# Warming matmuls in the first head, the third head's split a head later, and low parts and gather products in another order at the end of attention

## The chip, the cores and the metric

One core of a Trainium2 chip runs the whole program. The metric is the device time of one execution in microseconds (us), the median of three runs.

## The reference

Three layers are chained, all in float32. First comes an attention in which a query sees only the keys whose six sign bits agree with its own; then a mixture of eight experts, one expert for each token; then a gated block.

```python
q_bucket = np.sum(((q @ proj) > 0) * powers, axis=-1)       # 6 bits; the same for k
scores = scale * np.matmul(q, k.transpose(0, 1, 3, 2))
scores = np.where(q_bucket == k_bucket, scores, -1e9)
attn = softmax(scores) ; x = attn @ v                       # 2 x 8 heads, 768 x 64
e_idx = np.argmax(x @ w_gate, axis=1)                       # 1536 tokens, 8 experts
out[mask] = gate_w * eom * (np.maximum(x[mask] @ w1[e], 0.0) @ w2[e])
return ((out @ w_a) * (out @ w_b)) @ w_out
```

## The kernel before

**Heads and tiles.** Sixteen heads run one after the other, each in six tiles of 128 queries against 768 keys. A running number g counts the tiles of all heads, six to a head: tile 0 is the first of head 0, tile 6 the first of head 1, tile 12 the first of head 2. One turn of the loop over g emits, in this order: scores of tile g+1 (`scores`, lines 158 and 159), their row minimum and from it scale and bias of the exponential (`smax`, mm in line 164 and sb in line 165, on DVE), then work named below, then the transposes of tile g (`tposes`, line 186) in two halves, each copied from PSUM by ACT (line 190) or DVE (line 192). The exponential (`sexp`, line 173) runs on ACT and stands at one of three places of the turn, chosen by a table. Two PSUM buffers hold scores, two hold transposes. The product with v of a head (`av_step`, line 201) runs in the tiles of the next head, so head 0 has none.

**Buckets in the scores.** The bucket comparison rides in the scores' matmul: each head's tiles tq and tk hold 64 rows of q or k, rounded, and twelve rows of codes (64 to 75) that add a large number where bits agree. The residuals stand in bq and bk. A head is prepared in these steps: load x (q and k) and v by SyncE's DMA queue (`load`, lines 96 and 98, called three heads ahead in tile 1 of a head); `split_a` rounds q to tq and k to tk on ACT (line 103); `split_b` makes bq on DVE (line 115) with a POOL cast (line 116), and bk on POOL (lines 118 and 119); `hash_mm` (line 128) multiplies x by the projection; `hash_codes` makes all codes in one DVE row (code, line 142), and four DMAs of SyncE carry them into tq and tk (line 147). There are two x buffers: head h's x goes where head h-2's was.

**What sets the order.** It is written out by hand; each engine and SyncE's queue run their rows in the order of emission, and waits are put in where data or a buffer's reuse ask for them. The dictionary K (line 25) holds the places: 'sa' and 'sb' name tile and place of the two `split_a` and `split_b` calls for the head two ahead, 'sa0' and 'sb0' the same for heads 0 and 1; 'ev', 'ev0', 'ev1' say for each half of a tile whether ACT (0) or DVE (1) copies the transposes. `hash_codes(h + 1)` stands in tile 1 of head h. Small POOL copies into `held` only hold POOL's queue until a given row is done.

**The end of attention.** Expert 0's tokens are gathered on TensorE: tokens of the second half are multiplied by one-hot rows (`x0_hot`, `x0_add`, lines 399 and 406) into two PSUM tiles, one for columns 0 to 255 and one for 256 to 511; `x_split` prepares high and low parts of the tokens (lines 375 and 376, xh); `x0_evac` (lines 418 and 419) makes xh and xl for the first expert product `mm1` (lines 903 to 905). In between the router (`router`) finds each token's expert (rows rt_..., oh, ohl on DVE) and its slot by counting matmuls (lines 285 to 292), and POOL scatters the tokens to DRAM (line 428). `heat(n)` issues n small matmuls whose result is not used; the kernel before calls it ahead of tile 0 only.

Of the kernel before, what the change touches and what calls it, by code (L numbers as in the profile page):

```python
# [7 lines left out]
F32 = mybir.dt.float32  # L8
# [5 lines left out]
ALU = mybir.AluOpType  # L14
# [6 lines left out]
NT = 6  # L21
N, DM, E, FF, F2 = 1536, 512, 8, 1024, 1536
C = 224
GR = ((0, 6), (6, 4), (10, 2))
K = {'se': (2, 0, 2, 0, 2, 0), 'se0': (0, 1, 2, 1, 1, 2), 'ev': (0, 0, 0, 1, 0, 1, 0, 0, 0, 0, 1, 0), 'ev0': (0, 0, 0, 1, 0, 1, 0, 0, 0, 1, 0, 0), 'ev1': (0, 0, 0, 1, 0, 1, 0, 0, 0, 1, 0, 1), 'avl': (5,), 'oul': 0, 'hml': 0, 'hc': ((0, 0), (0, 2), (1, 1), (2, 1)), 'sa': ((0, 2), (2, 2)), 'sb': ((1, 0), (2, 2)), 'sa0': ((2, 2), (4, 1)), 'sb0': ((3, 2), (5, 0)), 'ext': (1, 0, 2, 4, 7, 8), 'hm0': 0, 'hc0': ((1, 0), (1, 2), (3, 0), (4, 1))}
C_ID, C_TRI, C_THR, C_REV, C_TOK, C_IOTA, C_BASE, C_SLOT = 0, 128, 256, 258, 266, 278, 279, 287
CW = C_SLOT + C
FAR = 1024.0
# [4 lines left out]
def attn_moe_kernel(ctx: ExitStack, tc: tile.TileContext, xin, cst, projd, wblk, wmoe, w2in, out):  # L33
    nc = tc.nc
    PE, ACT, DVE, POOL = nc.tensor, nc.scalar, nc.vector, nc.gpsimd
# [13 lines left out]
    wl = big.tile([128, 80], F32, name="wl")  # L49
# [38 lines left out]
    NHD = NB * NH  # L88
# [18 lines left out]
    def split_b(h, i, lo=0, n=S):  # L107
        copy = POOL.tensor_copy if h or i else ACT.copy
        x = X[h][:, i * S + lo:i * S + lo + n]
        if lo == 0:  # L110
            B[h, i] = tb.tile([128, S], F32R, tag="b" + "qk"[i], name="b" + "qk"[i])
        b = B[h, i][:, lo:lo + n]
        t = T[h, i].bitcast(F32)[:, lo:lo + n]
        if i == 0:
            DVE.scalar_tensor_tensor(out=b[:64], in0=x[:64], scalar=-0.125, in1=t[:64], op0=ALU.mult, op1=ALU.subtract)
            copy(b[64:], t[64:])  # L116
        else:
            (POOL if h else DVE).tensor_tensor(out=b[64:], in0=x[64:], in1=t[64:], op=ALU.subtract)
            copy(b[:64], t[:64])
# [247 lines left out]

    slot_of, XH = {}, {}

    def x_split(d, t0=6, n=6):  # L370
        if d not in XH:
            XH[d] = [tb.tile([128, 6, 128], F32R, tag="tb"[i] + "qk"[d % 2], name="xh") for i in range(2)]
        h, l = (a[:, t0 - 6:t0 - 6 + n] for a in XH[d])
        x = x_all[:, t0:t0 + n, d * 128:(d + 1) * 128]
        ACT.activation(h, x, ACTF.Copy)
        POOL.tensor_tensor(out=l, in0=x, in1=h.bitcast(F32), op=ALU.subtract)

    x0 = {}

# [222 lines left out]
    with tc.manual_schedule():  # L602
# [18 lines left out]
        DVE.tensor_scalar(out=pst[:, 6:12], in0=pst[:, 0:6], scalar1=-1.0, scalar2=None, op0=ALU.mult)  # L621
        DVE.tensor_scalar(out=pst[:, 32:38], in0=pst[:, 38:44], scalar1=-1.0, scalar2=None, op0=ALU.mult)
        warm = ps_t.tile([128, 512], F32, tag="t", name="warm")
        def heat(n):
            for i in range(n):
                PE.matmul(warm[:, :128], ones, ones, start=True, stop=True)

        heat(44)
        hash_mm(0, (2, 3))
# [22 lines left out]
        def set_up(k):  # L652
            if k == 0:
                split_b(1, 0)
                POOL.tensor_copy(held, pt_[0][:, 0:1])
            elif k == 1:
                split_b(1, 1)
            elif k == 2:
                POOL.memset(oh, 0.0)
                zero = wraw.tile([128, 512], F32, tag="wr0", name="zero")  # L660
                POOL.memset(zero, 0.0)
                zeros.append(zero)
                DVE.tensor_copy(tri, cs[:, C_TRI:C_TRI + 128])
            elif k == 5:
                DVE.tensor_scalar(
                    out=tokc.bitcast(I32)[:, :, 0], in0=cs[:, C_TOK:C_TOK + 12], scalar1=-float(E * C), scalar2=None,
                    op0=ALU.add,
                )
                DVE.tensor_scalar(
                    out=base2, in0=cs[:, C_BASE:C_BASE + 8], scalar1=1.0 / 128, scalar2=None, op0=ALU.mult  # L670
                )
# [3 lines left out]
        L = NHD - 1  # L675
# [7 lines left out]
        for g in range(NG):  # L683
            h, t = divmod(g, NT)
            if t == 1 and h + 3 < NHD:
                load(h + 3)
            if g + 1 < NG:
                scores(g + 1)
                smax(g + 1)
            if g < NT:  # L690
                set_up(g)
            if 2 * NT <= g < 2 * NT + (E * C + N) // 256:
                for i in (g - 2 * NT,):
                    nc.sync.dma_start(
                        out=xr[i * 256:(i + 1) * 256].rearrange("(p r) d -> p r d", p=128),
                        in_=zeros[0].unsqueeze(1).to_broadcast([128, 2, 512]),
                    )
            if g == 6 * NT:
                for n in range(4):
                    for part in range(2):  # L700
                        w_load(n, part)
            if g == 10 * NT + 1:
                r = router(0)
                todo = [r["s1"], r["s1b"], None, lambda: (r["s2"](), r["s2c"]()), r["s2b"], r["s4"], r["s4b"]]
                for f in r["sc"]:
                    todo += [f, None]
                todo += [r["s4c"], None, None, None, r["s3a"], None, r["s3b"], None, None, None, r["s5"]]
            early, late = [], []
            if h < L:
                if t == (1 if h else 0):  # L710
                    early.append(lambda: hash_mm(h + 1))
                if h:
                    for k in AV_AT.get(t, ()):
                        early.append(lambda k=k: av_step(h - 1, k))
                if h > 1 and t == 4:
                    (late if K["oul"] else early).append(lambda: o_out(h - 2))
            elif t < 3:
                av_step(h - 1, 2 * t)
                av_step(h - 1, 2 * t + 1)
                if t == 0:  # L720
                    o_out(h - 2)
                if t == 2:
                    o_evac(h - 1)
            elif t == 3:
                o_out(h - 1)
            else:
                k = 3 * (t - 4)
                av_group(h, qa, (k, k + 1, k + 2))
                if t == 5:
                    o_evac(h, qa)  # L730
            for f in early:
                f()
            if h and h < L and t == 5 and not K["avl"].count(5):
                o_evac(h - 1)
            if g > 10 * NT + 1 and todo:
                f = todo.pop(0)
                if f:
                    f()

            def side(pos):  # L740
                if g + 1 < NG and K["se" if 0 < h < L else "se0"][t] == pos:
                    sexp(g + 1)
                if h < L and (t, pos) == (1, 0):
                    hash_codes(h + 1)
                for i in range(2):
                    if h + 2 < NHD and K["sa" if h > 1 else "sa0"][i] == (t, pos):
                        split_a(h + 2, i)
                    if h + 2 < NHD and K["sb" if h > 1 else "sb0"][i] == (t, pos):
                        if t == 5:
                            POOL.tensor_copy(held, last[0])  # L750
                        split_b(h + 2, i)

            side(0)
            tposes(g, 0)
            side(1)
            tposes(g, 1)
            for f in late:
                f()
            if h and h < L and t == 5 and K["avl"].count(5):
                o_evac(h - 1)  # L760
            side(2)
            for f in extra.get((h - L + 1, t), ()):
                f()
        o_out(L, qa)
        av_group(L, qb, tuple(range(NT)))
        ra, rb = router(1), router(2)
        ra["s1"]()
        ra["s1b"]()
        x_split(3, 6, 4)
        x0_first(0, 3)  # L770
        ra["s2"]()
        x0_first(3, 8)
# [12 lines left out]
        rb["s1b"]()  # L785
        rb["s2"]()
        rb["s2p"]()
        x_split(3, 10, 2)
        x0_add(9)
        for t in (10, 11):  # L790
            x0_hot(DVE, t)
        x0_add(10)
        for i in range(2):
            x0_add(11, (2 * i, 2 * i + 1))
        rb["s2c"]()
        for f in ("s4", "s4b"):
            ra[f]()
# [109 lines left out]
        def mm1(e, f):  # L907
            wh, wl = W1.pop(e * 8 + f)
            xh, xl = XS[e]
            p = ph1.tile([128, 512], F32, tag="h", name="h1")  # L910
            for d in range(4):
                w = slice(d * 128, (d + 1) * 128)
                mm3(p[:, :C], wh[:, w], wl[:, w], xh[:, d], xl[:, d], d == 0, d == 3)
            hl = hp.tile([128, 2, C], F32R, tag="hl", name="hl")
            h, l = hl[:, 0], hl[:, 1]
            ACT.activation(h, p[:, :C], ACTF.Relu)  # L916
            DVE.scalar_tensor_tensor(  # L917
                out=l, in0=p[:, :C], scalar=0.0, in1=h.bitcast(F32), op0=ALU.max, op1=ALU.subtract
            )
            HT[e, f] = hl  # L920
# [421 lines left out]
```

## Time and profile before

| | |
|---|---|
| median of three runs | 741.0 us (740.35 to 744.32) |
| the profiled execution | 742.89 us, of it span 741.0 us |
| first expert product | from 261.96 us |
| TensorE busy | 723.9 us (98%) |
| VectorE (DVE), ScalarE (ACT), GpSimd (POOL) busy | 522.7, 434.8, 281.9 us |

A row of the timeline reads: start in us, duration in us, engine, source line, operation, output and inputs, size; in square brackets how long the engine had stood still before it, and what ended that. PE is TensorE, PEld its weight loads, SPq the rows of SyncE's DMA queue. PEclk is the granted clock of TensorE as a share of full speed.

### The profile page before, as it was taken

To read this page: it belongs to the slowest core of one execution; us is meant where nothing else is said; L and a number is where in the kernel's file an instruction comes from. 1 tells how busy PE (TensorE), PEld (TensorE's weight loads), DVE (VectorE), ACT (ScalarE), POOL (GpSimd) and SP (SyncE) were. 2 spreads that over 40 slices of the span, in tenths; PEclk is the share of its full clock that TensorE was granted. 3 is DMA by queue.
4 is the path that set the end of the run, shared out by engine and by line. 5 is a ranking of instruction groups with operands and counts; after the bars stand their busy time and mean duration, and the time that the engine had idled before them with its cause. 6 is when DMAs were issued, how large, how long until landed. Compare 5 with 4: busy or idle time off the path is not lost.

```text
span 741.0 us, 13428 instructions
## 1 busy us (share of the span) xinstructions
PE 723.9 (98%) x4621; PEld 623.4 (84%) x4622; DVE 522.7 (71%) x1034; ACT 434.8 (59%) x944; POOL 281.9 (38%) x321
## 2 busy tenths in 40 slices
PE   7999999999999999999999999999999999999995
PEld 6767777677766789999999999999999988999984
DVE  6777877888776769777889866778667245656641
ACT  5787787777786447766677744444544334344331
POOL 3232333223633374222111123535343466565543
PEclk9899999999999999999999999999999999999998
DMA  7347351231301048888897645555553331212102
GB/s 240 114 172 287 112 175 58 62 112 58 127 22 61 15 170 261 242 206 224 295 307 235 213 129 199 185 187 197 179 204 123 106 102 55 86 54 76 58 1 88
DMA packets 49594, 107.37 MB, mean 145 GB/s; under 512 B 8096, under 2 KB 11504, under 8 KB 47984
## 3 DMA queue, kind: packets, MB, share of 16 engines
q1 hardware_dynamic: 46848, 99.94, 41.6%
q0 software_dynamic: 2304, 6.31, 2.3%
q8 instruction: 38, 0.62, 0.4%
q14 instruction: 36, 0.29, 0.1%
q10 hardware_dynamic: 368, 0.20, 0.1%
HBM read 82.76 MB, written 22.56 MB: 142 GB/s over the span
## 4 chain that ended last, share of the span: by engine, by line
PE 87%; issue 3%; DVE 3%; ACT 2%; DMA 2%; POOL 2%; SPq 0%; ACTq 0%; POOLq 0%; DVEq 0%
PE tp L186 9%; PE av L201 8%; PE y L943 6%; PE s L158 4%; PE s L159 4%; PE acc L1065 4%; PE acc L1064 4%; PE acc L1066 4%; PE h L905 3%; PE h L904 3%; PE h L903 3%; PE y L944 3%; PE abb L903 2%; PE aba L904 2%; PE abb L904 2%
## 5 line engine op out<-in xcount | busy, mean ns | idle before, releaser
L164 DVE TENSOR_REDUCE mm<-s 128x1 f32<-128x768 f32 x96 | 91.1, 949 | 27.0 <-PE s L159 26.3
L173 ACT ACTIVATE p<-s,sb 128x768 f32<-128x768 f32 x96 | 94.9, 989 | 22.4 <-DVE sb L165 21.7
L862 POOL TENSOR_TENSOR pc<-t,pc 128x256 fp32r<-128x256 f32 x86 | 74.8, 892 | 83.6 <-ACT pc L861 83.6
L186 PEld LDWEIGHTS tp<-cs,p 128*128 128x128 f32 x576 | 65.9, 143 | 36.4 <-ACT p L173 23.1
L186 PE MATMUL tp<-cs,p 128*128 128x128 f32 x576 | 83.7, 282 | 4.9 <-ACT p L173 2.5
L485 DVE TENSOR_TENSOR wl<-wr,wh 128x512 fp32r<-128x512 f32 x125 | 81.0, 689 | 6.6 <-ACT wh L484 1.7
L190 ACT ACTIVATE pt<-tp 128x384 f32<-128x384 f32 x143 | 65.0, 487 | 33.6 <-PE tp L186 33.6
L943 PE MATMUL y<-hl,wh 128*128 128x448 f32 x224 | 75.0, 378 | 0.5 <-DVE hl L917 0.3
L484 ACT ACTIVATE wh<-wr 128x512 fp32r<-128x512 f32 x128 | 73.8, 624 | 2.9 <-DMA wr<-wmoe 2.8
L158 PE MATMUL s<-tk,tq 76*128 76x384 f32 x192 | 73.9, 385 | 0.3 <-DVE tq L135 0.3
L903 PE MATMUL h<-xh,wh 128*128 128x224 f32 x256 | 71.3, 279 | 0.2 <-ACT xh L418 0.2
L905 PE MATMUL h<-xh,wl 128*128 128x224 f32 x256 | 70.5, 276 | 0.0
L904 PE MATMUL h<-xl,wh 128*128 128x224 f32 x256 | 70.2, 274 | 0.3 <-DVE xl L419 0.3
L201 PE MATMUL av<-pt,v 128*64 128x384 f32 x360 | 68.0, 499 | 0.2 <-DVE r L225 0.2
L159 PE MATMUL s<-bk,bq 128*128 128x384 f32 x192 | 65.8, 343 | 0.0
L944 PE MATMUL y<-hl,wl 128*128 128x224 f32 x224 | 59.5, 266 | 0.0
L1064 PE MATMUL acc<-h,gh 128*128 128x512 f32 x144 | 56.7, 394 | 0.4 <-ACT gh L1050 0.4
L1065 PE MATMUL acc<-l,gh 128*128 128x512 f32 x144 | 56.8, 395 | 0.0
L1066 PE MATMUL acc<-h,gl 128*128 128x512 f32 x144 | 56.7, 393 | 0.0
L874 POOL TENSOR_TENSOR l<-t,h 128x512 fp32r<-128x512 f32 x24 | 31.1, 1296 | 65.0 <-ACT h L873 65.0
L116 POOL CAST bq<-tq 64x768 fp32r<-64x768 f32 x15 | 21.0, 1399 | 81.7 <-ACT tq L103 49.8
L916 ACT ACTIVATE hl<-h 128x224 fp32r<-128x224 f32 x64 | 22.8, 356 | 48.6 <-PE h L905 42.9
(226 smaller groups left out, 1889.4 us busy)
## 6 DMA issues: line engine op xcount, KB each, us to landing
wr<-wmoe SPq DMA_DIRECT2D x128, 256.0 KB
r<-w2in SPq DMA_DIRECT2D x12, 1536.0 KB
x<-xin SPq DMA_DIRECT2D x30, 384.0 KB
w<-t SPq DMA_DIRECT2D x36, 256.0 KB
t<-w SPq DMA_DIRECT2D x36, 256.0 KB
xr<-zero SPq DMA_DIRECT2D x13, 512.0 KB
xg<-xr SPq DMA_DIRECT2D x14, 256.0 KB
v<-xin SPq DMA_DIRECT2D x16, 192.0 KB
```

Of the source, the lines that this page charges most:

```text
L158: PE.matmul(p[:, c, :384], T[h, 0][:76, qs], T[h, 1][:76, sl], start=True, stop=False)
L159: PE.matmul(p[:, c, :384], B[h, 0][:, qs], B[h, 1][:, sl], start=False, stop=True)
L164: DVE.tensor_reduce(out=m[:, 1:2], in_=st[g][:, :, :384], axis=AX.XY, op=ALU.min)
L173: ACT.activation(p.rearrange("p (c n) -> p c n", c=2), st.pop(g)[:, :, :384], ACTF.Exp, scale=scl.pop(g), bias=nbs.pop(g), accum_out=sums[ ...
L186: PE.transpose(ps[:, j * 128:(j + 1) * 128], pt_[g][:, k * 128:(k + 1) * 128], ident)
L201: PE.matmul(av[h][c * 64:(c + 1) * 64, :384], v, PT[h][:, k, c * 384:(c + 1) * 384], start=(k == 0), stop=(k == NT - 1), skip_group_check= ...
L903: PE.matmul(ps, wh, xh, start=first, stop=False)
L904: PE.matmul(ps, wh, xl, start=False, stop=False)
L905: PE.matmul(ps, wl, xh, start=False, stop=last)
L943: PE.matmul(p, wh[:, w], hl, start=(f == 0), stop=False, skip_group_check=True)
L1064: PE.matmul(acc[i], h[:, w], wh, start=(f == 0), stop=False)
L1065: PE.matmul(acc[i], h[:, w], wl, start=False, stop=False)
```

## The change

Four things change. In turns g = 1 to 6, between the scores of tile g+1 and the transposes of tile g, four warming matmuls are issued into a PSUM tile `fill` of their own. Nothing is split in head 0 any more: in head 1, head 2 is split in tiles 0 to 2 and head 3 in tiles 3 to 5; from head 2 on all is as before. With that `hash_codes` stands in tile 3 of heads 0 and 1 instead of tile 1, a POOL copy into `held` puts head 1's bk behind sb of tile 2, and the second copy of tile 1's transposes goes from DVE to ACT ('ev1'). At the end of attention the two low parts of `x_split` go from POOL to DVE, at places of their own, and the last two gather products go by column halves. Last, the first expert product takes its matmuls by halves, with the low part of x last.

```diff
-K = {... 'ev1': (0, 0, 0, 1, 0, 1, 0, 0, 0, 1, 0, 1), ... 'sa': ((0, 2), (2, 2)), 'sb': ((1, 0), (2, 2)), 'sa0': ((2, 2), (4, 1)), 'sb0': ((3, 2), (5, 0)), ...}
+K = {... 'ev1': (0, 0, 0, 0, 0, 1, 0, 0, 0, 1, 0, 1), ... 'split': ((), ((1, ((0, 2), (2, 2)), ((1, 0), (2, 2))), (2, ((3, 2), (4, 1)), ((4, 2), (5, 0)))), ((2, ((0, 2), (2, 2)), ((1, 0), (2, 2))),)), ...}
...
-    def x_split(d, t0=6, n=6):
+    def x_split(d, t0=6, n=6, low=POOL):
...
-        POOL.tensor_tensor(out=l, in0=x, in1=h.bitcast(F32), op=ALU.subtract)
+        if low:
+            low.tensor_tensor(out=l, in0=x, in1=h.bitcast(F32), op=ALU.subtract)
+        return lambda: DVE.tensor_tensor(out=l, in0=x, in1=h.bitcast(F32), op=ALU.subtract)
...
             elif k == 1:
+                POOL.tensor_copy(held, last[0])
                 split_b(1, 1)
...
+            if 1 <= g <= NT:
+                if g == 1:
+                    fill = ps_a.tile([128, 512], F32, tag="a", name="fill")
+                heat(4, fill)
...
-                if h < L and (t, pos) == (1, 0):
+                if h < L and (t, pos) == (1 if h > 1 else 3, 0):
                     hash_codes(h + 1)
                 for i in range(2):
-                    if h + 2 < NHD and K["sa" if h > 1 else "sa0"][i] == (t, pos):
-                        split_a(h + 2, i)
...
+                    for n, sa, sb in K["split"][min(h, 2)]:
+                        if h + n < NHD and sa[i] == (t, pos):
+                            split_a(h + n, i)
...
         ra, rb = router(1), router(2)
+        low = x_split(3, 6, 4, None)
         ra["s1"]()
         ra["s1b"]()
-        x_split(3, 6, 4)
+        low()
...
-        x_split(3, 10, 2)
+        low = x_split(3, 10, 2, None)
         x0_add(9)
         for t in (10, 11):
             x0_hot(DVE, t)
-        x0_add(10)
+        low()
         for i in range(2):
-            x0_add(11, (2 * i, 2 * i + 1))
+            for t in (10, 11):
+                x0_add(t, (2 * i, 2 * i + 1))
...
+            if e == f == 0:
+                for i in range(2):
+                    for a, x in ((wh, xh), (wl, xh), (wh, xl)):
+                        for d in (2 * i, 2 * i + 1):
...
```

On DVE, tiles 2 to 4 before: mm and sb come once for each tile, pt is a copy of transposes, bq belongs to head 2, code to head 1.

```order
L164 TENSOR_REDUCE mm<-s 128x1
L165 SCALAR_TENSOR_TENSOR sb<-mm 128x2
L142 TENSOR_SCALAR code<-m,thr 128x384
L192 COPY pt<-tp 128x3x128
L164 TENSOR_REDUCE mm<-s 128x1
L165 SCALAR_TENSOR_TENSOR sb<-mm 128x2
L663 CAST tri<-cs 128x128
L192 COPY pt<-tp 128x3x128
L164 TENSOR_REDUCE mm<-s 128x1
L165 SCALAR_TENSOR_TENSOR sb<-mm 128x2
L115 SCALAR_TENSOR_TENSOR bq<-x,tq 64x768
```

And the same three tiles in the changed kernel:

```order
L164 TENSOR_REDUCE mm<-s 128x1
L165 SCALAR_TENSOR_TENSOR sb<-mm 128x2
L164 TENSOR_REDUCE mm<-s 128x1
L165 SCALAR_TENSOR_TENSOR sb<-mm 128x2
L666 CAST tri<-cs 128x128
L192 COPY pt<-tp 128x3x128
L164 TENSOR_REDUCE mm<-s 128x1
L165 SCALAR_TENSOR_TENSOR sb<-mm 128x2
L142 TENSOR_SCALAR code<-m,thr 128x384
```

Code moved from behind sb of tile 2 to behind sb of tile 4, two tiles ahead of the scores that need it; bq of head 2 left head 0.

On DVE, tiles 9 and 10 of head 1 before (bq is head 3's):

```order
L164 TENSOR_REDUCE mm<-s 128x1
L165 SCALAR_TENSOR_TENSOR sb<-mm 128x2
L192 COPY pt<-tp 128x3x128
L164 TENSOR_REDUCE mm<-s 128x1
L165 SCALAR_TENSOR_TENSOR sb<-mm 128x2
L115 SCALAR_TENSOR_TENSOR bq<-x,tq 64x768
```

And now (code is head 2's):

```order
L164 TENSOR_REDUCE mm<-s 128x1
L165 SCALAR_TENSOR_TENSOR sb<-mm 128x2
L192 COPY pt<-tp 128x3x128
L164 TENSOR_REDUCE mm<-s 128x1
L165 SCALAR_TENSOR_TENSOR sb<-mm 128x2
L142 TENSOR_SCALAR code<-m,thr 128x384
L164 TENSOR_REDUCE mm<-s 128x1
L165 SCALAR_TENSOR_TENSOR sb<-mm 128x2
L115 SCALAR_TENSOR_TENSOR bq<-x,tq 64x768
```

Head 2's code stands behind sb of tile 10. Its four DMAs keep their place in SyncE's queue, behind the load of head 4.

On TensorE, the last gather products and the start of the first expert product before (x is the PSUM tile of gathered tokens, hot the one-hot rows, h the product):

```order
L406 MATMUL x_3147<-hot,xh 128x224 x4
L406 MATMUL x_3148<-hot,xh 128x224 x4
L406 MATMUL x_3147<-hot,xh 128x224 x4
L406 MATMUL x_3148<-hot,xh 128x224 x4
L903 MATMUL h_3355<-xh,wh_2844 128x224
L904 MATMUL h_3355<-xl,wh_2844 128x224
L905 MATMUL h_3355<-xh,wl_2845 128x224
```

And now:

```order
L408 MATMUL x_3172<-hot,xh 128x224 x8
L408 MATMUL x_3173<-hot,xh 128x224 x8
L925 MATMUL h_3380<-xh,wh_2869 128x224 x2
L925 MATMUL h_3380<-xh,wl_2870 128x224 x2
L925 MATMUL h_3380<-xl,wh_2869 128x224 x2
```

The first PSUM tile is complete eight matmuls earlier, and the low part xl is needed by the fifth matmul of the product instead of the second.

## Rows read from the trace of the kernel before

**Rows 1.** The page, busy time, share of the span and instructions of each engine.

```profile
PE 723.9 (98%) x4621; PEld 623.4 (84%) x4622; DVE 522.7 (71%) x1034; ACT 434.8 (59%) x944; POOL 281.9 (38%) x321
```

**Rows 2.** Windows (PE: stretch, length, busy, count, granted clock, DMA share, GB/s); timeline, twenty warming matmuls.

```profile
19.20:19.60 0.40, 0.00 (x0) 0.51 0.89 334
20.00:25.00 5.00, 5.00 (x21) 0.50 0.07 20
25.80:26.20 0.40, 0.40 (x5) 0.71 0.00 0
...
7.60 1.29 PE L626 MATMUL warm<-ones 128*128 128x128 bf16 x20
```

**Rows 3.** Timeline, TensorE: transposes of tiles 2 to 5, ends of scores 6, 12.

```profile
17.52 0.87 PE L186 MATMUL tp<-cs,p 128*128 128x128 f32 x6 [1.49 <-ACT p L173]
19.69 1.54 PE L186 MATMUL tp<-cs,p 128*128 128x128 f32 x6 [0.59 <-ACT p L173]
22.31 1.48 PE L186 MATMUL tp<-cs,p 128*128 128x128 f32 x6
24.55 0.52 PE L159 MATMUL s<-bk,bq 128*128 128x384 f32 x1
27.49 0.88 PE L186 MATMUL tp<-cs,p 128*128 128x128 f32 x6 [0.46 <-ACT p L173]
39.06 0.34 PE L159 MATMUL s<-bk,bq 128*128 128x384 f32 x1
```

**Rows 4.** Timeline, POOL's cast and DVE's sb of tiles 2 and 4.

```profile
15.51 0.82 POOL L119 CAST bk<-tk 64x768 fp32r<-64x768 f32 x1
15.70 0.65 DVE L165 SCALAR_TENSOR_TENSOR sb<-mm 128x2 f32<-128x2 f32 x1
20.20 0.16 DVE L165 SCALAR_TENSOR_TENSOR sb<-mm 128x2 f32<-128x2 f32 x1
```

**Rows 5.** Timeline, POOL's bk of head 1, SyncE's queue, code of head 2.

```profile
13.62 1.83 POOL L118 TENSOR_TENSOR bk<-x,tk 64x768 fp32r<-64x768 f32 x1
19.09 1.47 SPq L147 DMA_DIRECT2D tk<-code  x2
29.96 0.81 SPq L96 DMA_DIRECT2D x<-xin  x2
30.41 0.68 DVE L142 TENSOR_SCALAR code<-m,thr 128x384 fp32r<-128x384 f32 x1
31.35 1.52 SPq L147 DMA_DIRECT2D tq<-code  x2
32.92 1.47 SPq L147 DMA_DIRECT2D tk<-code  x2
```

**Rows 6.** Windows (stretch, length, granted clock, DMA share, GB/s): last code data of head 1.

```profile
21.20:21.40 0.20, 0.50 0.39 85
21.40:21.60 0.20, 0.50 0.04 8
```

**Rows 7.** Timeline, ACT's exponential of tile 9 and next split, DVE's sb of tile 10.

```profile
34.17 0.99 ACT L173 ACTIVATE p<-s,sb 128x768 f32<-128x768 f32 x1 [0.50 <-DVE sb L165]
35.16 0.83 ACT L103 ACTIVATE tq<-x 128x768 fp32r<-128x768 f32 x1
...
35.97 0.16 DVE L165 SCALAR_TENSOR_TENSOR sb<-mm 128x2 f32<-128x2 f32 x1 [0.56 <-DVE mm L164]
```

**Rows 8.** Timeline, end of attention; page, the group of DVE's 128x512 subtractions.

```profile
252.69 1.27 POOL L376 TENSOR_TENSOR xh<-x_all,xh 128x512 fp32r<-128x512 f32 x1 [7.66 <-ACT xh L375]
252.96 1.04 DVE L279 TENSOR_TENSOR oh<-rt_cd,rt_cm 128x32 bf16<-128x32 f32 x1
262.62 0.37 PE L904 MATMUL h<-xl,wh 128*128 128x224 f32 x1 [0.28 <-DVE xl L419]
...
L485 DVE TENSOR_TENSOR wl<-wr,wh 128x512 fp32r<-128x512 f32 x125 | 81.0, 689 | 6.6 <-ACT wh L484 1.7
```

**Rows 9.** Waits of SyncE's queue, 225 to 300 us (total, times, longest); timeline, ACT.

```profile
SPq L883 <- DMA xr<-x_all,pos_i: 25.7, 2, 24.5
...
277.03 1.26 ACT L484 ACTIVATE wh<-wr 128x512 fp32r<-128x512 f32 x2 [2.35 <-DMA wr<-wmoe]
```

More of the change, by code (lines that the diff above doesn't have):

```diff
@@ L24 @@
 GR = ((0, 6), (6, 4), (10, 2))
-K = {'se': (2, 0, 2, 0, 2, 0), 'se0': (0, 1, 2, 1, 1, 2), 'ev': (0, 0, 0, 1, 0, 1, 0, 0, 0, 0, 1, 0), 'ev0': (0, 0, 0, 1, 0, 1, 0, 0, 0, 1, 0, 0), 'ev1': (0, 0, 0, 1, 0, 1, 0, 0, 0, 1, 0, 1), 'avl': (5,), 'oul': 0, 'hml': 0, 'hc': ((0, 0), (0, 2), (1, 1), (2, 1)), 'sa': ((0, 2), (2, 2)), 'sb': ((1, 0), (2, 2)), 'sa0': ((2, 2), (4, 1)), 'sb0': ((3, 2), (5, 0)), 'ext': (1, 0, 2, 4, 7, 8), 'hm0': 0, 'hc0': ((1, 0), (1, 2), (3, 0), (4, 1))}
+K = {'se': (2, 0, 2, 0, 2, 0), 'se0': (0, 1, 2, 1, 1, 2), 'ev': (0, 0, 0, 1, 0, 1, 0, 0, 0, 0, 1, 0), 'ev0': (0, 0, 0, 1, 0, 1, 0, 0, 0, 1, 0, 0), 'ev1': (0, 0, 0, 0, 0, 1, 0, 0, 0, 1, 0, 1), 'avl': (5,), 'oul': 0, 'hml': 0, 'hc': ((0, 0), (0, 2), (1, 1), (2, 1)), 'split': ((), ((1, ((0, 2), (2, 2)), ((1, 0), (2, 2))), (2, ((3, 2), (4, 1)), ((4, 2), (5, 0)))), ((2, ((0, 2), (2, 2)), ((1, 0), (2, 2))),)), 'ext': (1, 0, 2, 4, 7, 8), 'hm0': 0, 'hc0': ((1, 0), (1, 2), (3, 0), (4, 1))}
 C_ID, C_TRI, C_THR, C_REV, C_TOK, C_IOTA, C_BASE, C_SLOT = 0, 128, 256, 258, 266, 278, 279, 287
@@ L623, in attn_moe_kernel, with heat @@
         warm = ps_t.tile([128, 512], F32, tag="t", name="warm")
-        def heat(n):
+        def heat(n, p=warm):
             for i in range(n):
-                PE.matmul(warm[:, :128], ones, ones, start=True, stop=True)
+                PE.matmul(p[:, :128], ones, ones, start=True, stop=True)
         heat(44)
@@ L742, in side @@
                     sexp(g + 1)
-                if h < L and (t, pos) == (1, 0):
+                if h < L and (t, pos) == (1 if h > 1 else 3, 0):
                     hash_codes(h + 1)
                 for i in range(2):
-                    if h + 2 < NHD and K["sa" if h > 1 else "sa0"][i] == (t, pos):
-                        split_a(h + 2, i)
[L748 to L751, printed above, removed]
+                    for n, sa, sb in K["split"][min(h, 2)]:
+                        if h + n < NHD and sa[i] == (t, pos):
+                            split_a(h + n, i)
+                        if h + n < NHD and sb[i] == (t, pos):
+                            if t == 5:
+                                POOL.tensor_copy(held, last[0])
+                            split_b(h + n, i)
             side(0)
@@ L910, in mm1 @@
             p = ph1.tile([128, 512], F32, tag="h", name="h1")
-            for d in range(4):
-                w = slice(d * 128, (d + 1) * 128)
-                mm3(p[:, :C], wh[:, w], wl[:, w], xh[:, d], xl[:, d], d == 0, d == 3)
+            if e == f == 0:
+                for i in range(2):
+                    for a, x in ((wh, xh), (wl, xh), (wh, xl)):
+                        for d in (2 * i, 2 * i + 1):
+                            PE.matmul(
+                                p[:, :C], a[:, d * 128:(d + 1) * 128], x[:, d], start=(d == 0 and a is wh and x is xh),
+                                stop=(d == 3 and x is xl),
+                            )
+            else:
+                for d in range(4):
+                    w = slice(d * 128, (d + 1) * 128)
+                    mm3(p[:, :C], wh[:, w], wl[:, w], xh[:, d], xl[:, d], d == 0, d == 3)
             hl = hp.tile([128, 2, C], F32R, tag="hl", name="hl")
```

## The prediction

> **What bounds the kernel now.** I read the page first. TensorE is busy 98% of the span [rows 1], so time is gained only where TensorE waits or runs slowly, and any new wait of TensorE is added in full. The edits touch heads 0 and 1 and the join of attention and experts. I then read the granted clock by stretch, the timeline of 9 to 48 us and of 250 to 282 us, and the waits of the DMA queue.
>
> In head 0 there is nothing to multiply by v yet, so TensorE has gaps. It stood 1.49 us ahead of tile 2's transposes [rows 3] and again ahead of tile 3's; at 19.2 us the granted clock fell from full (2.4 GHz) to 0.51 and 0.50 (1.2 GHz), and it came back at about 26 us, after more than 6 us of unbroken work (5.00 us busy of the 5.00 from 20 to 25) [rows 2]. In that stretch a tile took 2.62 us (19.69 to 22.31), and six transposes took 1.48 us instead of 0.88 [rows 3]. Tile 2 is late for another reason: its DVE row sb (the scale and bias of the exponential) took 0.65 us, where tile 4's took 0.16, and ended with a POOL cast (16.33) [rows 4]; then came code, 0.68 us on DVE (its row of head 2 in [rows 5]).
>
> I number tiles g through all heads; scores of tile 6 are the first of head 1, those of tile 12 the first of head 2. A head's first scores read the twelve code rows that four DMAs write into that head's tq and tk. In the kernel before these DMAs have finished long before. That slack is what this change spends.
>
> **The change part by part.**
>
> *Warming matmuls.* Six times four matmuls of 128 columns. Twenty of them take 1.29 us [rows 2], so four take 0.26 us. They stand between the scores and the transposes of a tile, where TensorE waits for the exponential (1.49 us ahead of tile 2, 0.59 us ahead of tile 3 [rows 3]); tiles without that wait pay at most 0.26 us. If they keep the clock, the three tiles from 19.69 to 27.49 save some 0.45 us each (2.62 against the 2.17 from 17.52 to 19.69 [rows 3]), 1.3 us. With the cast and code gone from tile 2, another 0.5 us. Up to 1.8 us, then, if nothing else comes late. Something does.
>
> *Codes of head 1.* They move from ahead of tile 1's copy to behind sb of tile 4. That sb ended at 20.36 [rows 4]; with the 0.5 us of tile 2, 19.9. Code then ends at 20.6. The DMA queue needs 0.26 us to its first issue (31.09 to 31.35) and 3.04 us for the four (to 34.39), the third ending 0.74 us sooner [rows 5]; the last one's data were in SBUF 0.9 us or more behind its issue (20.56 to about 21.5) [rows 5, 6]. So the third has landed at 24.1 and the fourth at 24.8 at the earliest. TensorE would have come to tile 6 at about 21.8; it waits some 2.3 us, does half of the scores, and ends them at about 25.3 or later. In the kernel before they ended at 25.07 [rows 3]. So the whole gain of head 0 goes into this wait: +0.4 us net (0 to +0.8; the upper end for a semaphore that fires later than the data).
>
> The Trainium skill, "DMA: Bandwidth & Descriptors", section on the anatomy of one DMA, puts the fixed part of a DMA at about 2.0 us, most of it the receipt of the last write; it measured that on the other issue path. With 2.0 in place of the 0.9 both waits for codes would be 1.1 us longer, and the sum 2.2 us. The rows show when data moved, not when the semaphore fired, so nothing here decides it.
>
> *Head 2's split a head later, and its codes.* This is the large term. The queue on SyncE is in order, and its order is unchanged: in head 1 the load of head 4's x (two DMAs) and v stands ahead of the four code DMAs. Head 4's x goes into the buffer of head 2's x, so it waits until everything has read that. Before, head 2 was split in head 0 and the load went out at once. Now the last reader is POOL's k residual (bk) of head 2, and this waits for ACT's tk, which stands behind the exponential of tile 9. Step by step, on the clock of the kernel before: that exponential starts at 34.17 and ACT is free at 35.16; tk takes 0.83 us (as the tq row there), to 36.0; POOL's residual 1.83 us, to 37.9 [rows 5, 7]. From the end of that POOL operation to the end of the seventh issue (two x, v, four codes) the kernel before shows this very chain in head 0: 15.45 to 20.56, 5.1 us; at the pace of head 1 it is 4.4 us (29.96 to 34.39) [rows 5]. So the last code DMA is issued by 42.3 to 43.0 and its data are in by 43.2 to 43.9. The scores of tile 12, whose second half needs it, ended at 39.40 before [rows 3]; they now end 0.4 us behind the data, at 43.6 to 44.3. That is +4.2 to +4.9 us; I take **+4.6**, near the faster pace's middle. Queued behind these scores on TensorE are the product with v and every later tile, and nothing in PE-bound heads gives it back. ACT and DVE do two heads' splits in head 1; both have room inside this wait, so I cost that at nothing.
>
> *The clock behind the waits.* A gap of 1.49 us and a shorter one were enough for half clock before [rows 2, 3]; one of about 4 us ahead of tile 12 should do no less, and there no warming matmuls stand. Half clock then lasted 6.3 us of work, of which 40% is lost (1 - 0.88/1.48 [rows 3]): 2.5 us. Bounds 0 and 3.0; I take +2.0, as part of it falls into the gap itself. For the 2.3 us gap ahead of tile 6: 0 to +2.0, in a stretch with waits of its own; I take +0.8.
>
> *End of attention.* The low part of x for head 6 and 7's columns moves from POOL (1.27 us) to DVE. DVE's row oh took 1.04 us and ended as that POOL row did; without it I give it 0.19 us, as sb of tile 4 took 0.16 where nothing held it [rows 4, 8]. DVE gains 0.85 us and pays about 0.7 us for the low part (its 128x512 subtractions average 0.689 us [rows 8]), so DVE is even and TensorE's counting matmuls start about 0.5 us earlier. The reordered gather (tile 10 and 11 by halves) and the first expert product, which now takes the low part of x last, remove the 0.28 us wait there [rows 8] and part of the evacuation ahead of it; up to 1.1 us in all. But the experts then run into a transfer: weights stand in the same queue behind loads that waited for POOL's scatters (24.5 us, the longest wait of that queue), and ACT's split of them, at 277.03, starts on their landing [rows 9]; TensorE's next product uses it. The scatters start from DVE rows that move by 0.1 to 0.3 us only (0.5 earlier, less 0.4 for the second low part). So -0.2 us (0 to -1.1).
>
> **Sum.** +0.4 +0.8 +4.6 +2.0 -0.2 = +7.6 us. The profiled execution took 742.89 us, of which 741.0 was span; the median of three runs is 741.0, so the change counts against that: 741.0 + 7.6 = **748.6 us**. With every bound at its low end but the wait, 741 + 0 + 0 + 4.2 + 0 - 1.1 = 744.1; at the high end, 741 + 0.8 + 2.0 + 4.9 + 3.0 = 751.7.
>
> **The rivals.**
>
> *The change does what it says (faster).* The mechanism: warm transposes and scores in head 0, with code rows in time. Price: -1.8 us in head 0, -0.2 to -1.1 us at the end: 738 to 739. For it speaks the half clock in rows 2, which is really there. Against it speaks the arithmetic of the queue: it decides only if the codes of head 2 are in SBUF by 39 us, and they can't be while a POOL operation that ends at 37.9 gates seven issues of 0.4 to 0.75 us. It needs issues four times as fast as any in rows 5. Even then it is a gain of 0.3%. 0.10.
>
> *The x load is not in the way.* If head 4's load goes out early (were its wait on another operation), the codes follow sb of tile 10: 36.13 [rows 7] + 0.68 + 0.26 + 3.04 + 0.9 = 41.0, scores end at 41.4: +2.0 in place of 4.6, and the clock may hold: 741 + 0.4 + 2.0 - 0.2 + 0 to 1 = 743.2 to 744.2. The buffer's reuse in the code speaks against it. 0.13.
>
> *The warming isn't enough.* If the clock falls at 19.2 us as before, the gap ahead of tile 6 closes from the other side: TensorE arrives late and the codes are there. Net of head 0 +0.5 to +1 us instead of +1.2: 748 to 749, the same forecast by another road; it is part of its range.
>
> *Worse.* Both gaps cost full half-clock stretches and the semaphores fire late: above 752. 0.05.
>
> **How the numbers follow.** About 0.5% (3.7 us) is what a measurement of this kernel can tell from no change. The forecast, 744.1 to 751.7, has 0.72. The x-load rival with 0.13 lies at 743.2 to 744.2, within 0.5%; the faster rival with 0.10 lies at 738 to 739, also within 0.5%, of which I give 0.03 to more than 0.5%. Slower by over 0.5% (above 744.7): 0.72 less a little at its low edge plus 0.05, so 0.75. Within 0.5%: 0.22. Faster: 0.03. The range from 743.2 to 751.8 holds the forecast and the second rival, 0.85 on paper, and I leave it there because the clock term is the least certain.
>
> **What the profile afterwards would show.** Right: SyncE's x load of head 1 starting on POOL's bk residual at about 38 us, the code issues ending past 42 us, TensorE idle 4 us ahead of tile 12's scores with a DMA of tk named as releaser, an idle of about 2 us ahead of tile 6's, and a granted clock of 0.5 behind the longer one. From about 60 us on, everything is a copy shifted by 7 to 8 us; at the join TensorE is earlier by up to 1 us against attention's end and gives it back by 280 us. Wrong: scores of tile 12 without such a wait, or code DMAs ahead of the x load. If the wait is there and the clock at 1.00 behind it, the sum is 2 us too high.

## The result and the profile after

The changed kernel takes 751.66 us (median of four, 751.15 to 753.65), the kernel before beside it 741.11. The ratio is 1.0143, with a 95% interval of 1.0121 to 1.0166: **10.5 us slower**, where 7.6 were forecast. The profiled execution of the changed kernel took 751.69 us, of which 749.9 was span. The page's busy times (us, share of the span, instructions) have hardly changed from [rows 1]: TensorE's grew by 1.7 us, while the span grew by 8.9 us. Most of the loss is waiting. A part is work at half clock, which this comparison hides, since the first profile of the kernel before had half clock of its own: in its second profile (run 3) TensorE is busy 721.4 us, 4.2 less than here (the warming matmuls are in that too).

```profile
PE 725.6 (97%) x4645; PEld 623.0 (83%) x4646; DVE 521.9 (70%) x1035; ACT 434.9 (58%) x945; POOL 281.1 (37%) x319
```

I then read the waits of TensorE over the first 330 us (engine, line and what it waited for: us in total, times, longest):

```profile
PE s L158 <- DMA tk<-code: 7.1, 2, 5.1
```

Of the other waits one matters, 2.21 us for expert 1's tokens (xg) at the join; it comes below. The two waits for codes stand where the prediction put them, and neither was in the first profile of the kernel before. The rows of TensorE around them, with the hash matmuls (L128) of heads 1, 2 and 3 as milestones:

```profile
10.20 0.85 PE L128 MATMUL m<-x,pst 128*32 128x384 f32 x8
...
23.64 0.42 PE L158 MATMUL s<-tk,tq 76*128 76x384 f32 x1 [2.03 <-DMA tk<-code]
...
25.47 1.49 PE L186 MATMUL tp<-cs,p 128*128 128x128 f32 x6
...
29.63 0.85 PE L128 MATMUL m<-x,pst 128*32 128x384 f32 x8
...
43.99 0.66 PE L158 MATMUL s<-tk,tq 76*128 76x384 f32 x1 [5.11 <-DMA tk<-code]
...
45.53 2.83 PE L201 MATMUL av<-pt,v 128*64 128x384 f32 x8
...
51.17 0.85 PE L128 MATMUL m<-x,pst 128*32 128x384 f32 x8
```

Tile 12's scores, which ended at 39.40 before [rows 3], begin at 43.99. Behind both waits the same operations take 1.7 to 1.9 times as long: six transposes 1.49 us, as in [rows 3] at half clock, and the product with v 2.83 us where it took 1.51 in other heads. The windows say the same (stretch, length, busy, count, granted clock, DMA share, GB/s):

```profile
23.00:27.00 4.00, 3.32 (x15) 0.67 0.03 6
...
45.00:47.00 2.00, 2.00 (x8) 0.50 0.31 116
```

What held the codes of tile 12 is in the rows of DVE, POOL and SyncE's queue:

```profile
36.60 0.68 DVE L142 TENSOR_SCALAR code<-m,thr 128x384 fp32r<-128x384 f32 x1 [0.45 <-issue]
...
36.62 1.83 POOL L118 TENSOR_TENSOR bk<-x,tk 64x768 fp32r<-64x768 f32 x1 [3.66 <-ACT tk L103]
...
38.48 0.81 SPq L96 DMA_DIRECT2D x<-xin  x2
...
39.87 1.53 SPq L147 DMA_DIRECT2D tq<-code  x2
41.44 1.47 SPq L147 DMA_DIRECT2D tk<-code  x2
```

Code was ready at 37.28. The load of x waited for POOL's bk (end 38.45), took the queue at 38.48, and the codes' four DMAs stood behind it until 42.9.

From hash row to hash row, head 1 takes 21.54 us (29.63 to 51.17), against 14.84 (29.01 to 43.85) in the first profile of the kernel before; head 2 takes 14.55 and 14.56. Head 0 takes 19.43 us (10.20 to 29.63), against 18.21 (10.80 to 29.01). The rows of the first profile, with the first scores of tile 6:

```profile
10.80 0.85 PE L128 MATMUL m<-x,pst 128*32 128x384 f32 x8
...
23.44 0.67 PE L158 MATMUL s<-tk,tq 76*128 76x384 f32 x1
...
29.01 0.85 PE L128 MATMUL m<-x,pst 128*32 128x384 f32 x8
...
43.85 0.85 PE L128 MATMUL m<-x,pst 128*32 128x384 f32 x8
```

At the join, rows of DVE, the queue and TensorE:

```profile
260.58 0.19 DVE L279 TENSOR_TENSOR oh<-rt_cd,rt_cm 128x32 bf16<-128x32 f32 x1
...
278.81 1.47 SPq L893 DMA_DIRECT2D xg<-xr  x2
...
284.31 0.44 PE L904 MATMUL xt<-cs,xg 128*128 128x128 f32 x2 [2.21 <-DMA xg<-xr]
```

From the logits of the last tiles (L245) to the second expert product is 12.96 us (257.81 to 270.77), against 13.76 before (250.18 to 263.94): 0.80 us gained. Part of it is oh, 1.04 us beside POOL's subtraction in [rows 8] and 0.19 without it, as estimated. Then TensorE stands still for 2.21 us until expert 1's tokens have come.

### The profile page after: what moved, and what is told of

It is laid out like the page before. It is cut to its first block, busy times and chain, and to the rows that moved or that the text cites. A ratio compares the mean times of both kernels' runs of the same rounds, so it can differ in the third digit from the quotient of the medians.

```text
span 749.9 us, 13477 instructions
## 1 busy us (share of the span) xinstructions
PE 725.6 (97%) x4645; PEld 623.0 (83%) x4646; DVE 521.9 (70%) x1035; ACT 434.9 (58%) x945; POOL 281.1 (37%) x319
## 4 chain that ended last, share of the span: by engine, by line
PE 87%; issue 3%; DVE 3%; DMA 2%; POOL 2%; ACT 1%; SPq 1%; ACTq 0%; POOLq 0%; DVEq 0%
PE tp L186 9%; PE av L201 9%; PE y L962 6%; PE s L158 4%; PE s L159 4%; PE acc L1084 4%; PE acc L1083 4%; PE acc L1085 4%; PE h L915 3%; PE h L913 3%; PE h L914 3%; PE y L963 3%; PE abb L913 2%; PE aba L914 2%; PE abb L914 2%
```

## The experiments

All ratios are to the kernel before, run beside each.

**1. Only the end of attention.** The kernel before with the last three parts of the diff (low parts on DVE, gather products by halves, first product by halves).

> The kernel before with only the edits at the end of attention (low parts of x on DVE, the last gather products by column halves, the first expert product by halves). In the changed kernel the second expert product started 0.8 us earlier against attention's end, and then TensorE waited 2.2 us for a gather load of expert 1 (xg). Theory 1: the 0.8 us is gained and given back at that load, because the load stands behind POOL's scatters and these are only 0.2 us earlier: 740.9 to 741.3 without a slow transfer, 742 to 743 if the same 2.2 us wait comes. Theory 2 (the xg wait comes from the shift of the whole program, not from these edits): no wait of TensorE for xg, 740.3 to 741.0.

Measured: 741.28 us, ratio 1.0004 (0.9993 to 1.0014). TensorE's rows at the gather of expert 1:

```profile
272.02 0.44 PE L898 MATMUL xt<-cs,xg 128*128 128x128 f32 x2 [0.65 <-DMA xg<-xr]
```

TensorE comes earlier and waits for xg (0.65 us here and 0.21 at the next pair), as theory 1 has it; the time is that of theory 1 without a slow transfer. These edits are worth nothing that can be measured.

**2. The changed kernel without the split's move.** The warming matmuls and the end of attention are left:

```diff
-'split': ((), ((1, ...), (2, ...)), ...)
+'sa': ..., 'sb': ..., 'sa0': ((2, 2), (4, 1)), 'sb0': ((3, 2), (5, 0))
-                POOL.tensor_copy(held, last[0])
-                if h < L and (t, pos) == (1 if h > 1 else 3, 0):
+                if h < L and (t, pos) == (1, 0):
```

> The changed kernel with the third head's split, the codes and POOL's held copy where they were before: warming matmuls and the edits at the end of attention are left. If the codes behind the x load are what costs (theory 1), TensorE waits for no code in tiles 6 and 12, the granted clock stays at 1.00 from 19 to 26 us, head 0 ends 1.0 to 1.8 us earlier than before, and the time is 739 to 740.5 (2 us more if the wait for xg comes again). If the warming matmuls themselves cost (theory 2: 24 matmuls at 0.1 us in TensorE's path, and no clock gained), it is 742 to 744.

Measured: 741.56 us, ratio 1.0005 (0.9995 to 1.0015), which neither theory gives. The waits for codes are gone, and the clock is 1.00 from 19 to 27 us, but nothing is gained against run 1, which has no warming. Why is seen in run 1's rows of the same place, then in this run's:

```profile
10.46 0.85 PE L128 MATMUL m<-x,pst 128*32 128x384 f32 x8
...
20.66 0.93 PE L186 MATMUL tp<-cs,p 128*128 128x128 f32 x6 [0.52 <-ACT p L173]
...
21.78 0.42 PE L158 MATMUL s<-tk,tq 76*128 76x384 f32 x1 [0.19 <-DMA tk<-code]
...
26.65 0.85 PE L128 MATMUL m<-x,pst 128*32 128x384 f32 x8
```

```profile
11.06 0.85 PE L128 MATMUL m<-x,pst 128*32 128x384 f32 x8
...
21.27 0.93 PE L186 MATMUL tp<-cs,p 128*128 128x128 f32 x6 [0.28 <-ACT p L173]
...
26.98 0.85 PE L128 MATMUL m<-x,pst 128*32 128x384 f32 x8
```

Run 1 has head 0 as in the kernel before, and its clock did not fall either: six transposes take 0.93 us at 20.66, where [rows 3] show 1.48 and 1.54. The warming matmuls only fill part of a wait for the exponential (0.52 becomes 0.28). Head 0 takes 16.19 us in run 1, 15.92 with warming, and 15.92 without it too in the next run. The third row of run 1 is the first of tile 6's scores: even with the codes in their old place, TensorE waits 0.19 us for them.

**3. The kernel before, a second time.** Runs 1 and 2 put the half clock of [rows 2] in doubt, so the unchanged kernel was profiled again.

> The kernel before, unchanged, profiled a second time. Theory 1 (the half clock of 19 to 26 us in its first profile belongs to that execution, whose mean clock of 0.992 is below the 0.994 to 0.998 of 23 others): granted clock 1.00 in that stretch, mean 0.995 to 0.998, the hash matmuls of head 2 at 26.5 to 27.5 us instead of 29.01, 740 to 742. Theory 2 (it belongs to the kernel): the clock falls again and the row stands at 29.

Measured: 740.25 us, mean clock 0.997. The timeline of TensorE and DVE, then the window of 19 to 27 us:

```profile
11.14 0.85 PE L128 MATMUL m<-x,pst 128*32 128x384 f32 x8
...
15.74 0.16 DVE L165 SCALAR_TENSOR_TENSOR sb<-mm 128x2 f32<-128x2 f32 x1
...
22.18 0.42 PE L158 MATMUL s<-tk,tq 76*128 76x384 f32 x1
...
27.06 0.85 PE L128 MATMUL m<-x,pst 128*32 128x384 f32 x8
```

```profile
19.00:27.00 8.00, 6.41 (x40) 1.00 0.18 62
```

Theory 1 holds. Head 0 takes 15.92 us here (11.14 to 27.06) and 18.21 in the first profile. In that one the transposes of tile 0 had waited 1.46 us for the DMA of cs, POOL's cast lay on tile 2's sb (0.65 us in [rows 4], 0.16 here, the row at 15.74), and the clock fell. Tile 6's scores begin 11.04 us behind the hash row here (11.14 to 22.18), 12.64 in the first profile. The mean clock of the first profile was 0.992; in the 23 timed runs of the kernel before beside runs 1 and 2 it is 0.994 to 0.998. The 2.3 us belong to that execution.

**4. Only the split's move.** The kernel before with the new places of splits, codes and the held copy.

> The kernel before with only the move of the third head's split, of the codes and the held copy; no warming, end of attention as before. Theory 1 (the two waits for codes are the whole loss up to 60 us, and the warming gave nothing since what it gained went into the wait ahead of tile 6): transposes that stood at 50.4 us before and at 57.7 in the changed kernel stand at 57.5 to 58.5, and the time is 748 to 749.5. Theory 2 (warming is worth its 1 to 1.8 us): 59 us or later, 750 and more.

Measured: 752.36 us, ratio 1.0140 (1.0118 to 1.0162), the changed kernel's loss. The time is that of theory 2, but not for its reason, as the rows show:

```profile
13.51 0.96 PE L186 MATMUL tp<-cs,p 128*128 128x128 f32 x6 [2.46 <-DMA cs<-cst]
...
25.48 0.42 PE L158 MATMUL s<-tk,tq 76*128 76x384 f32 x1 [2.02 <-DMA tk<-code]
...
30.75 0.85 PE L128 MATMUL m<-x,pst 128*32 128x384 f32 x8
...
45.28 0.66 PE L158 MATMUL s<-tk,tq 76*128 76x384 f32 x1 [5.29 <-DMA tk<-code]
...
53.42 0.85 PE L128 MATMUL m<-x,pst 128*32 128x384 f32 x8
```

This execution lost another 1.1 us to the DMA of cs (2.46 against 1.33) and, behind it, clock; and its half clock behind tile 12 lasts longer (8.14 us from 45.28 to the hash row, against 7.18 from 43.99). So the waits are those of the changed kernel; what warming is worth can't be read from this pair.

**5. Head 4's load behind the codes.** The changed kernel with one line:

```diff
-            if t == 1 and h + 3 < NHD:
+            if t == (4 if h == 1 else 1) and h + 3 < NHD:
                 load(h + 3)
```

> The changed kernel with one edit: in head 1 the load of head 4's x and v is issued in tile 4 instead of tile 1, so that it stands behind the four code DMAs of head 2 in SyncE's queue. Theory 1 (queue order): code ends at 37.3 us as now, the four DMAs are issued from 37.5 to 40.6 and land by 41.5 instead of 43.8; TensorE's wait ahead of tile 12 falls from 5.1 to 2.3 to 2.8 us, 2.3 to 3.0 us are saved in all: 748.5 to 749.5. Theory 2 (the loss is the work of two splits in head 1, or a DMA that is slow wherever it stands): wait unchanged at 5 us, 751 to 752.

Measured: 748.96 us, ratio 1.0112 (1.0083 to 1.0140). The queue (the last two code DMAs; the x load comes behind them, at 40.91), and on TensorE tile 12's scores between the hash rows of heads 2 and 3:

```profile
30.03 0.85 PE L128 MATMUL m<-x,pst 128*32 128x384 f32 x8
...
39.33 1.48 SPq L147 DMA_DIRECT2D tk<-code  x2
...
41.36 0.44 PE L158 MATMUL s<-tk,tq 76*128 76x384 f32 x1 [2.09 <-DMA tk<-code]
...
48.60 0.85 PE L128 MATMUL m<-x,pst 128*32 128x384 f32 x8
```

The wait falls from 5.11 to 2.09 us, and head 1 from 21.54 to 18.57 (30.03 to 48.60). Theory 1 holds: 3 us of the loss are the order of the queue. The single runs lie between 745.8 and 753.3 us, in the order of their mean clock, 0.997 to 0.985, and the interval of the ratio overlaps that of the changed kernel: it is the wait that shows the 3 us, not the time.

**6. Only the codes moved.** The kernel before with the codes of heads 1 and 2 in tile 3; the split stays, so the x load has its buffer early.

> The kernel before with one edit: the codes of heads 1 and 2 in tile 3 instead of tile 1. Head 2 is split in head 0 as before, so the load of head 4's x has its buffer early. Theory 1 (the split's move costs only through the queue): waits of about 2 us ahead of tiles 6 and 12, as in the changed kernel with the load behind the codes, and its time: 746 to 749. Theory 2 (two splits in one head cost something themselves): 744 to 745.5, less than that kernel.

Measured: 748.08 us, ratio 1.0095 (1.0080 to 1.0111).

```profile
24.61 0.66 PE L158 MATMUL s<-tk,tq 76*128 76x384 f32 x1 [2.18 <-DMA tk<-code]
...
31.13 0.85 PE L128 MATMUL m<-x,pst 128*32 128x384 f32 x8
...
42.67 0.41 PE L158 MATMUL s<-tk,tq 76*128 76x384 f32 x1 [2.22 <-DMA tk<-code]
...
49.83 0.85 PE L128 MATMUL m<-x,pst 128*32 128x384 f32 x8
```

Head 1 takes 18.70 us with one split in it, 18.57 in run 5 with two. The work of the second split costs nothing itself: theory 1.

**7. Warming in the waits.** The changed kernel with warming matmuls where TensorE waits for codes:

```diff
         st[g] = p
+        for _ in range({6: 24, 12: 72}.get(g, 0)):
+            PE.matmul(p[:, 0, :128], ones, ones, start=True, stop=True)
```

> The changed kernel with 24 warming matmuls ahead of tile 6's scores and 72 ahead of tile 12's (into the PSUM tile that the scores then write), 1.55 and 4.6 us of work inside the waits of 2.03 and 5.11 us. Theory 1 (half clock behind the waits costs 2.0 and 0.8 to 1.2 us): granted clock 1.00 from 19 to 60 us, waits for codes as long as before, 748.5 to 749.3. Theory 2 (the clock behind the waits costs next to nothing, or falls whatever is issued): 751 to 752.

Measured: 748.50 us (747.39 to 751.35), ratio 1.0101 (1.0086 to 1.0117). The profiled execution is the slowest of the four, with 3.15 us of wait for cs ahead of tile 0 and half clock behind that; its head 1 can be read:

```profile
27.14 0.42 PE L160 MATMUL s<-tk,tq 76*128 76x384 f32 x1 [0.97 <-DMA tk<-code]
...
32.42 0.85 PE L128 MATMUL m<-x,pst 128*32 128x384 f32 x8
...
46.60 0.42 PE L160 MATMUL s<-tk,tq 76*128 76x384 f32 x1 [0.92 <-DMA tk<-code]
...
51.85 0.85 PE L128 MATMUL m<-x,pst 128*32 128x384 f32 x8
```

Its window of 45 to 47 us, the columns as above:

```profile
45.00:47.00 2.00, 1.08 (x15) 1.00 0.26 80
```

The codes come as late as ever and the clock stays at 1.00. Head 1 takes 19.43 us: 4.59 over the 14.84 of before, without a clock term. From the scores of tile 12 to the hash row it is 5.25 us here and 7.18 in the changed kernel: half clock cost 1.93 us there. Behind tile 6 the same two rows give 5.28 (27.14 to 32.42) against 5.99, 0.71 us. Theory 1 holds.

**8. Codes of head 1 early.** Run 5 with head 1's codes back in tile 1 of head 0:

```diff
-                if h < L and (t, pos) == (1 if h > 1 else 3, 0):
+                if h < L and (t, pos) == (3 if h == 1 else 1, 0):
```

> The changed kernel with head 4's load in tile 4 of head 1 (behind the code DMAs, as in the run before this) and head 1's codes back in tile 1 of head 0; head 2's codes stay in tile 3, since its split ends in tile 2. Theory 1 (each wait for codes is the distance between code and scores, less the DMA chain): no wait ahead of tile 6, 2.1 us ahead of tile 12 as with the load alone moved, half clock behind that one only: 2.0 + 0.4 us of wait and about 1 us of half clock less, 744 to 746. Theory 2 (head 0 is slowed by something else, as its POOL copy): tile 6 late all the same, 747 to 749.

Measured: 747.15 us, ratio 1.0089 (1.0073 to 1.0104), above theory 1's band. Half of the wait ahead of tile 6 is still there. POOL, the queue, and TensorE:

```profile
16.37 0.18 POOL L659 COPY held<-sb 128x1 f32<-128x1 f32 x1 [2.15 <-DVE sb L165]
16.64 1.80 POOL L118 TENSOR_TENSOR bk<-x,tk 64x768 fp32r<-64x768 f32 x1
...
18.47 0.80 SPq L96 DMA_DIRECT2D x<-xin  x2
...
23.74 0.41 PE L158 MATMUL s<-tk,tq 76*128 76x384 f32 x1 [1.01 <-DMA tk<-code]
```

Code had ended at 16.83, but its first DMA is issued at 19.86: head 3's x goes into head 1's buffer, its load waits for head 1's bk, and the change puts that behind the held copy. I had not seen this second chain: in the changed kernel code itself came later (it ended at 19.76) and hid it.

**9. The same without the held copy.**

```diff
             elif k == 1:
-                POOL.tensor_copy(held, last[0])
                 split_b(1, 1)
```

> The run with head 1's codes in tile 1, less the POOL copy into held ahead of head 1's bk. There that copy put bk behind sb of tile 2, and the load of head 3's x, which reuses head 1's x buffer and stands ahead of head 1's code DMAs, started at 18.47 us and the codes' first DMA at 19.86, though code had ended at 16.8. Theory 1 (the same queue once more, one head earlier): without the copy the x load starts at 15.7 to 16.4, the codes are issued by 21.0, the wait of 1.01 us ahead of tile 6 is 0 to 0.2, one us is saved: 745.5 to 746.5. Theory 2 (the wait came from another thing): unchanged, 747 to 748.

Measured: 746.33 us, ratio 1.0071 (1.0054 to 1.0088).

```profile
15.58 1.48 SPq L96 DMA_DIRECT2D x<-xin  x2
...
22.19 0.41 PE L158 MATMUL s<-tk,tq 76*128 76x384 f32 x1 [0.22 <-DMA tk<-code]
```

The codes' first DMA is now issued at 17.64. Theory 1 holds by the wait; the time alone, 0.8 us less, does not tell this run from run 8 (the intervals overlap). Head 0 is back at 16.22 us (10.91 to 27.13), as in run 1. Of the 5.5 us that are left, 3.7 are head 1 (18.58 us, 27.13 to 45.71, against 14.84): tile 12's wait of 2.1 us with its half clock, since the program issues head 2's codes behind its split, which ends in tile 2. An earlier place for them was not tried. The other 1.7 us aren't separated; a wait of 2.01 us for xg is among the rows of this execution. No version here beats the kernel before.

## Why the prediction was right, and where it was 3 us short

**The direction and the large term were right.** Head 2's codes behind the x load were put at +4.6 us (+2.0 if only their own later place counts) and the clock behind that wait at +2.0. Head 1 is 6.70 us longer (21.54 less 14.84); 1.93 of that is clock by run 7, 4.77 the wait, and run 7, without half clock, shows 4.59. Run 5 takes the load out of the way and 3 us go, where the prediction's 4.6 less 2.0 says 2.6. The clock behind tile 6 was put at +0.8 and measures 0.71 in this execution; in run 4 it didn't fall there, so the closeness of that figure is luck.

**The step that failed is the one on warming**, and with it the net of head 0. I took 1.8 us as there to be gained (1.3 of clock, 0.5 of tile 2's late sb) and set them against the wait ahead of tile 6, so that +0.4 was left. Run 3 shows that both belong to the one execution that was profiled: head 0 takes 15.92 us, not 18.21. Against 15.92 the changed kernel's 19.43 is +3.51, or 2.8 without the clock behind tile 6, in place of +0.4. Against the first profile it is +1.22, which is the +0.4 and +0.8 of the sum. So I took a gain from an execution of 742.89 us and set it against a median of 741.0, in which most of it was already contained.

The chain of the codes itself came out as forecast: tile 6's scores were to begin 13.3 us behind head 1's hash row (24.1 less 10.80) and begin 13.44 behind it. What they were compared with was wrong. The prediction says that these DMAs have finished long before. That holds for tile 12, and for tile 6 in the first profile only, where a late start and half clock had made the scores late; in run 1 TensorE waits 0.19 us for them. There was no slack to spend ahead of tile 6: the first tk issue of head 1's codes stands 8.35 us behind the hash row in run 3 (19.49) and 11.32 in the changed kernel (21.52), 2.97 us later, and head 0 pays 2.8 of it. A late sb was there again too, one tile on: behind the held copy POOL's bk of head 1 (15.52 to 17.33) runs beside tile 3's sb, which takes 0.79 us (16.56 to 17.35).

3.51 + 6.70 is 10.2 us, beside a difference of the medians of 10.5. The spans of the two profiled executions differ by 11.5 us (749.9 and 738.4): their start gives -0.9, heads 0 and 1 together +10.2, the heads behind +0.3, and all from the join's logits on +1.9. So the closeness of 10.2 to 10.5 is chance in part. The result lies at the top end of the range, which held it by 0.14 us through bounds that were made for other terms.

**The landing of the codes** was sized a little short. I took a semaphore at 0.9 us or more behind the end of an issue of some 0.7 us, 1.6 in all. In run 5 the scores start 2.03 us behind the start of the tk issue (39.33 to 41.36), in run 6 2.10, in run 9 2.04; in the changed kernel, right behind the x load, 2.55 (41.44 to 43.99). Run 7, with the x load ahead too, has 2.38 and run 4 2.73, so one figure does not cover all. The Trainium skill, "DMA: Bandwidth & Descriptors", in the section on the anatomy of one DMA, gives about 2.0 us as the fixed part, setup included, measured on the other issue path; the rows without the load ahead agree with it, counted from the start of the issue. The prediction had tried it behind the issue's end, which made each wait 1.1 us longer; the landing came 0.4 us later than its 1.6.

**Two splits in one head** were costed at nothing: right (18.57 against 18.70 in run 6).

**The end of attention**, -0.2 us (0 to -1.1): run 1 gives a change of -0.5 to +1.0 us by its interval. That the gain would be given back was right; the place was half right. It is TensorE's own wait for xg, whose loads are issued right ahead of the weights that I named. The four profiles with the old order wait 0 to 0.87 us there, the seven with the new one 0.79 to 2.22 (2.21 in the changed kernel, 0.86 in run 1, 2.01 in run 9). From the logits of the last tiles to the end of the span the old order takes 490.2 to 491.3 us, the new one 490.5 to 492.8, on average 0.8 more: if anything these edits cost, but run 1's interval holds both signs. Why one transfer takes so much longer than another was not tried. The gain is also smaller than the text on the change suggests: in the rows given there the first PSUM tile of the gather is complete four matmuls earlier, not eight.

**The rivals.** Run 6 is the case in which the x load isn't in the way. I priced it at 743.2 to 744.2; it took 748.1, since its price had the same +0.4 for head 0 and hardly any clock. The case in which the change does what it says had little to win: run 2 has the warming without the wait, and takes the same time as before. The rival in which the warming isn't enough did not occur in the changed kernel, whose granted clock is 1.00 from 19 to 23 us, ahead of the wait. *Worse* came within 0.4 us: the median is 751.66, and one run took 753.65.

## What to carry to other kernels

A stall is worth removing only if it stands in more than one execution: where the profiled run is slower than the median or its mean clock lower than that of the others, look for a second profile before the stall's price goes into a sum against the median. The same holds for slack: what looks like room ahead of a reader may be only that this execution's reader came late. When work moves to a later place, follow its last reader: a buffer that comes free later holds the load that reuses it, and every transfer that stands behind that load in an in-order queue.

## What the runs showed that was not expected

- The start differs between executions. The transposes of tile 0 waited for the DMA of cs 1.33 us in the changed kernel, 1.46 in the first profile of the kernel before, 2.46 in run 4 and 3.15 in run 7; in the other runs it had landed in time. In the three with 1.46 us or more the granted clock fell in head 0 ahead of any wait for codes (0.72 as the mean of 13 to 19 us in runs 4 and 7, 0.50 to 0.51 from 19.2 us in [rows 2]), in run 7 with the warming matmuls behind the gap.
- A wait of about 2 us for codes was followed by half clock at tile 12 in runs 5, 6, 8 and 9 (7.16 to 7.24 us from the scores to the hash row, 5.25 without), and not at tile 6 in run 4 (5.27 us, where full speed gives 5.28). The Trainium skill, "TensorE: Matmul & The Clock Gate", part 1, says of a kernel's start that the number of slow matmuls differs from run to run of one kernel; that mean clock and time differ between run 5's six executions (0.985 to 0.997) is of the same kind, further inside the kernel.
